# Linear attention's queries multiplied by two heads at once, the features' high part over their low part, against sums with high and low side by side

## The chip, the cores and the metric

One core of one Trainium2 chip runs the whole program. Its engines are TensorE (PE), VectorE (DVE), ScalarE (ACT), GpSimd (POOL) and SyncE (SP, which here issues the DMAs). The metric is the device time of one execution in microseconds. Three executions of the kernel before took 955.29, 956.08 (the median) and 1325.11 us.

## What is computed

Two kinds of layers alternate, each behind a layer norm and with a residual: A, B, A, B over x of 2048 rows and 512 columns. A is linear attention with 32 heads of 16 columns, B a hidden layer of 1792 with relu. All weights and the input are float32.

```
def A(x):                          # x: 2048 x 512
    q, k, v = x @ wqkv             # 32 heads of 16
    pq, pk = q @ w_phi, k @ w_phi  # per head
    phi_q = concat(softmax(pq), softmax(-pq))   # 32 features of a head
    phi_k = concat(softmax(pk), softmax(-pk))
    kv = phi_k.T @ v;  z = sum(phi_k)           # per head: 32 x 16, 32
    o = (phi_q @ kv) / (phi_q @ z + 1e-6)
    return o @ wo
def B(x):
    return relu(x @ w1) @ w2
x = x + A(norm(x)); x = x + B(norm(x)); x = x + A(norm(x)); x = x + B(norm(x))
```

## The kernel before

Rows are handled in 16 chunks of 128; two chunks make a tile of 256 rows for layer B. TensorE multiplies float16 operands. A float32 operand is split into a high float16 part and a low one (the rest after rounding), and a product is made of three matmuls, high x high, high x low, low x high (`PAIRS`).

A layer A needs two passes. In the first, `keys` and `values` project each chunk (`project`, line 656; results `pk`, `pv`), `feature_map` makes the features, and `gather` adds the outer products of features and values to the sums of all heads (`kv`). `query` projects the queries (`pq`) and stores them. `summary` then masks the sums (line 989), splits them into `rhs0` (high) and `rhs1` (low): for each group of four heads a matrix of 128 features and 68 columns, 64 for the four heads' values and 4 for their denominators. In the second pass `look` loads a chunk's queries, makes their features `p16` (high and low, 1024 columns each), and a transposing DMA turns these into `pT`: 8 blocks of high parts and 8 of low ones, a block being four heads' 128 features by 128 rows. `numerators` (line 1079) multiplies, in two halves of four groups; each group takes three matmuls of 68 columns that add up in PSUM (`pn`). DVE adds the guard to the denominators, inverts them and multiplies (lines 1087, 1090, 1091) into `o`. `turn` splits `o` (ACT line 570, POOL line 573) into `n_o`, and a DMA (line 584) transposes it to `oT`; the first two chunks of a layer are transposed on PE instead (`fast`). `back_project` multiplies by `wo` (`pw`), then come the norm and layer B: `ph` are hidden sums, `py` outputs. Most tiles of layer B use seven products instead of eight (line 1495); ACT copies partial hidden sums out of PSUM there (`sn`, line 1508) before PE adds the next product. The second pass of a layer runs inside layer B's steps: `sides` puts the numerators and the back projection of a later chunk between the hidden matmuls of an earlier tile. In the first layer, the second layer's keys and values are also made there.

The opening: `wk` is first multiplied by the per-head matrix (`fold`). The raw weight `st_k` arrives in three pieces (two row blocks, one, one). PE transposes its sixteen 128x128 blocks (line 1805) into four banks by column group, ACT and DVE copy them (`wT_k`, lines 1811 and 1812), PE multiplies (`pf_k`, line 1847), ACT and DVE round and split the result (`wk_h`, `wk_l`). The scale of that split comes from the sum of squares of the raw weight (ACT line 391, `sb_k` on PE), through DVE, a power of -0.5 on POOL (line 410) and DVE (`root`). Chunks 0 to 3 of the first layer have their normalised rows transposed on PE (`tr_a`, line 599), all others by DMA (`xT<-n_a`).

Work is first listed as tasks with what they read and write; then each engine's order is taken from the table `ORDER`: a string for each engine, whose digits say which of the tasks that are left comes next. Each engine, and SP with its DMAs, runs its tasks strictly in that order, waiting where an operand is not there.

## Time and profile before

| | |
|---|---|
| median of three executions | 956.08 us (955.29 to 1325.11) |
| the profiled execution | 955.23 us, its span 953.5 us |
| mean granted clock of TensorE | 1.00 |
| DVE, ACT, POOL busy | 72%, 62%, 65% of the span |
| DMA | 183.39 MB, mean 192 GB/s; the main queue's packets take 73.2% of 16 engines' span |

In rows of the profile, a group's entry reads: line, engine, operation, output <- inputs, shapes, count | busy us, mean ns of one | idle time of the engine before them and who ended it. Rows of the chain and of the timeline begin with the start and the length in us. A matmul's own length includes the time in which it drains while the next one runs, so the distance between starts is what it costs PE. PEld is PE's weight load.

### The profile page before, as it was taken

To read this page: it belongs to the slowest core of one execution; us is meant where nothing else is said; L and a number is where in the kernel's file an instruction comes from. 1 tells how busy PE (TensorE), PEld (TensorE's weight loads), DVE (VectorE), ACT (ScalarE), POOL (GpSimd) and SP (SyncE) were. 2 spreads that over 40 slices of the span, in tenths; PEclk is the share of its full clock that TensorE was granted. 3 is DMA by queue.
4 is the path that set the end of the run, shared out by engine and by line. 5 is a ranking of instruction groups with operands and counts; after the bars stand their busy time and mean duration, and the time that the engine had idled before them with its cause. 6 is when DMAs were issued, how large, how long until landed. Compare 5 with 4: busy or idle time off the path is not lost.

```text
span 953.5 us, 23741 instructions
## 1 busy us (share of the span) xinstructions
PE 944.3 (99%) x9364; PEld 657.6 (69%) x9364; DVE 685.9 (72%) x1419; ACT 593.4 (62%) x1193; POOL 622.0 (65%) x666
## 2 busy tenths in 40 slices
PE   8999999999999999999999999999999999999998
PEld 5544545665675666667677875566666989888997
DVE  7999888677768768776476678986887665555445
ACT  8999888754564646455266555566566566565553
POOL 2697966768975847665177747256557888786554
PEclk9999999999999999999999999999999999999999
DMA  9488647569878598967849663688999977765442
GB/s 340 127 263 190 176 122 187 124 143 211 235 169 241 152 225 222 228 167 206 198 146 273 232 221 91 194 217 209 251 215 254 242 170 170 195 169 154 142 140 79
DMA packets 251840, 183.39 MB, mean 192 GB/s; under 512 B 180688, under 2 KB 188112, under 8 KB 251728
## 3 DMA queue, kind: packets, MB, share of 16 engines
q1 hardware_dynamic: 251728, 181.87, 73.2%
q8 instruction: 73, 1.20, 0.5%
q14 instruction: 39, 0.32, 0.1%
HBM read 108.30 MB, written 30.15 MB: 145 GB/s over the span
## 4 chain that ended last, share of the span: by engine, by line
PE 96%; ACT 1%; DMA 1%; DVE 0%; issue 0%; POOL 0%; POOLq 0%; SPq 0%; DVEq 0%
PE ph L1495 24%; PE py L1614 15%; PE py L1684 13%; PE pw L656 9%; PE pv L656 9%; PE pq L656 9%; PE pk L656 9%; PE ph L1575 4%; PE pn L1079 2%; PE kv L864 1%; DMA oT<-n_o 0%; DMA st_k<-in_A_wqkv_dram 0%; PE pv L843 0%; PE pf_q L1847 0%; PE tr_a L599 0%
## 5 line engine op out<-in xcount | busy, mean ns | idle before, releaser
L1508 ACT ACTIVATE sn<-ph 128x128 f32<-128x128 f32 x294 | 80.6, 275 | 152.6 <-PE ph L1495 149.5
L1614 PE MATMUL py<-w,h 128*128 128x512 f16 x690 | 174.2, 379 | 0.0
L1495 PEld LDWEIGHTS <-s 128*128 128x128 f16 x2352 | 151.4, 98 | 26.0 <-issue 1.3
L656 PEld LDWEIGHTS <-xT 128*128 128x128 f16 x900 | 87.0, 98 | 98.9 <-issue 1.0
L1495 PEld LDWEIGHTS <-w 128*128 128x128 f16 x1764 | 111.0, 98 | 13.2 <-DVE h L1225 0.6
L1495 PE MATMUL ph<-yT,s 128*128 128x128 f16 x1176 | 97.6, 219 | 0.9 <-DVE ph L1514 0.9
L1495 PE MATMUL ph<-yT,w 128*128 128x128 f16 x1176 | 97.6, 219 | 0.0
L1514 DVE TENSOR_TENSOR ph<-ph,sn 128x128 f32<-128x128 f32 x98 | 29.3, 299 | 94.5 <-PE ph L1495 48.2
L1614 PEld LDWEIGHTS <-h 128*128 128x128 f16 x690 | 61.4, 98 | 48.3
L771 POOL TENSOR_TENSOR p_q<-e_q,p_q 128x1024 f16<-128x1024 f32 x32 | 70.7, 2210 | 28.5 <-ACT p_q L767 28.5
L771 POOL TENSOR_TENSOR p_k<-e_k,p_k 128x1024 f16<-128x1024 f32 x30 | 66.7, 2222 | 24.2 <-ACT p_k L767 23.9
L656 PE MATMUL pk<-wk_h,xT 128*128 128x512 f16 x256 | 81.5, 379 | 0.0
L656 PE MATMUL pw<-wo_h,oT 128*128 128x512 f16 x256 | 81.2, 379 | 0.2 <-DMA oT<-n_o 0.2
L656 PE MATMUL pv<-wv_h,xT 128*128 128x512 f16 x256 | 81.2, 379 | 0.0
L760 POOL TENSOR_TENSOR e_k<-e_k,fm_k 128x1024 f32<-128x1024 f32 x30 | 59.3, 1977 | 32.3 <-ACT fm_k L752 32.1
L1519 DVE TENSOR_TENSOR ph<-ph,sn 128x256 f32<-128x256 f32 x98 | 41.9, 427 | 32.6 <-PE ph L1495 32.1
L1684 PEld LDWEIGHTS <-h 128*128 128x128 f16 x648 | 59.1, 98 | 7.5 <-issue 0.5
L656 PEld LDWEIGHTS <-oT 128*128 128x128 f16 x384 | 36.6, 98 | 39.9 <-DMA oT<-n_o 0.7
L1291 POOL TENSOR_TENSOR w<-r 128x256 f32<-128x256 f32 x41 | 32.5, 793 | 43.9 <-ACT r L1287 43.8
L656 PE MATMUL pq<-wq_h,xq 128*128 128x512 f16 x168 | 56.8, 379 | 0.2 <-ACT qs L933 0.2
L1684 PE MATMUL py<-w,h 128*128 128x256 f16 x324 | 53.0, 273 | 0.3 <-POOL w L1291 0.3
L1225 DVE SCALAR_TENSOR_TENSOR h<-ph,h 128x512 f16<-128x512 f32 x58 | 39.3, 681 | 18.8 <-ACT h L1222 18.8
(285 smaller groups left out, 2438.0 us busy)
## 6 DMA issues: line engine op xcount, KB each, us to landing
s<-s_dram SPq DMA_DIRECT2D x98, 512.0 KB, 4.5
q_dram<-qs SPq DMA_DIRECT2D x28, 256.0 KB, 3.2
ql<-q_dram SPq DMA_DIRECT2D x28, 256.0 KB, 3.8
u<-t_dram SPq DMA_DIRECT2D x13, 512.0 KB, 5.5
xt_dram<-xT SPq DMA_DIRECT2D x21, 256.0 KB, 4.4
xq<-xt_dram SPq DMA_DIRECT2D x21, 256.0 KB, 3.3
xe<-in_A_x_dram SPq DMA_DIRECT2D x16, 256.0 KB, 4.3
x<-in_A_x_dram SPq DMA_DIRECT2D x16, 256.0 KB, 5.0
```

The lines of the kernel that those rows point to most:

```text
L656: nc.tensor.matmul(pm.ap, xT.ap[:, a, k, :], W.ap[b][:, k, :], start=(k == 0 and i == 0), stop=(k == KC - 1 and i == 2))
L760: (nc.vector if fast else nc.gpsimd).tensor_tensor(e3, e3, sm.unsqueeze(2).to_broadcast([P, 2 * n, DH]), op=ALU.mult)
L771: (nc.vector if fast else nc.gpsimd).tensor_sub(part16(1, cols), part16(1, cols, ef), part16(0, cols))
L1225: add(DVE, 0.607, lambda: nc.vector.scalar_tensor_tensor(h[1].ap, at(), 0.0, h[0].ap, op0=ALU.max, op1=ALU.subtract), reads=[ph, h[0]], wr ...
L1291: nc.gpsimd.tensor_sub(rf.ap[:, :2, :], r.ap.rearrange("p (a b) -> p a b", a=4)[:, ::3, :], block(1).unsqueeze(1).to_broadcast([P, 2, P]))
L1495: nc.tensor.matmul(at(r), weight_of(i, b, kk, s, summed), rows_of(y, i, a, kk), start=(first and kk == 0 and n == 0), stop=(kk == 1 and n ...
L1508: nc.scalar.activation(saved(i), at(2), AF.Copy)
L1514: add(DVE, 0.27, lambda: nc.vector.tensor_tensor(at(3), at(1), saved(2), op=ALU.add), reads=[(ph, 1), (sn, 2)], writes=[(ph, 3)], boost=10 ...
L1519: add(DVE, 0.40, lambda: nc.vector.tensor_tensor(wide(ph), wide(ph), wide(sn), op=ALU.add), reads=[(sn, 0), (sn, 1)], writes=[(ph, 0), (ph ...
L1575: nc.tensor.matmul(at()[:, j, cs.start * P:cs.stop * P], W1.at(b, k, slice(f * P, (f + 1) * P)), yT.ap[:, cs, a, k, :], stop=(k == KC - 1 ...
L1614: nc.tensor.matmul(py.ap, h[a].ap.rearrange("p j t -> p (j t)")[:, cols], W2.at(b, fs[j], slice(0, D)), start=(begins and j == k == 0), st ...
L1684: nc.tensor.matmul(py.ap[:, 256 * r:256 * r + 256], left[a], right[b], start=(s == 0 and r == 0 and k == 0), stop=(last and k == 2 and not ...
```

## The change

Numerators. The features of the queries are laid out so that one transposed block holds two heads: 64 rows of high parts over 64 rows of low parts, 16 blocks for a chunk. `rhs` has, for each pair of heads, the sums twice over on the partitions (once for the high, once for the low features) and 68 columns: 34 of the sums' high part (32 values and 2 denominators) beside 34 of their low part. One matmul of a block gives (high + low) x high in the left 34 columns and (high + low) x low in the right 34; DVE adds the two sides by a reduction. So 16 matmuls of 68 columns take the place of 24, in three banks (6, 5 and 5 pairs) instead of two. The division is no longer taken from PSUM: after the join, ACT scales the denominators, POOL adds the guard, DVE inverts, POOL multiplies; in the second layer from chunk 10 on DVE does both POOL steps. The first two chunks of a layer (`numerators_at_once`) add the two sides on PE instead, with two matmuls of 34 columns for each pair into one place, 32 for a chunk, and divide from PSUM as before. `spread` reads the heads from tiles with 34 columns to a pair. The masks and the matrix that doubles the sums over the halves of the partitions are built for pairs in the opening (two more ACT copies and a DVE reduction, while the first weight is still on its way).

Opening. The transposes of `st_k` are made in four units of four, one bank each; each unit is copied by one instruction of 512 columns (DVE, ACT, DVE, DVE). The power of -0.5 is replaced by integer arithmetic on DVE (`root`). Chunks 2 and 3 are transposed by DMA (`fast=c < 2`).

Order. All five strings of `ORDER` are new. The core of the diff:

```diff
@@ ORDER, PE @@
-        "0000222222110104100001100070088006600413318011593473108302a0302901a02211013517002060013GG00E1D4420133140"
...
+        "0000222200000100007b090077000440300115307015810209302901a302110135006001612031F0514BB2A24031033003304706"
...
@@ root @@
         def bound():
+            total = pb.ap[:, :1]
             if sq.n > 1:
+                total = m.ap
                 nc.vector.tensor_reduce(m.ap, pb.ap[:, :sq.n], axis=AX.X, op=ALU.add)
-            nc.vector.tensor_scalar(m.ap, m.ap if sq.n > 1 else pb.ap[:, :1], 2.0 ** -80, None, op0=ALU.max)
+            if name == "phi":
+                nc.vector.tensor_scalar(m.ap, total, 2.0 ** -80, None, op0=ALU.max)
+                total = m.ap
+            nc.vector.tensor_scalar(m.ap.bitcast(I32), total.bitcast(I32), -0.5, float(0x5F3759DF),
+                                    op0=ALU.mult, op1=ALU.add)
+            nc.vector.tensor_scalar(pw.ap.bitcast(I32), m.ap.bitcast(I32), 0x7F800000, None, op0=ALU.bitwise_and)
 
         add(PE, 0.23, sums, reads=[sq], makes=[pb])
-        add(DVE, 0.3 if sq.n > 1 else 0.12, bound, reads=[pb], writes=[m])
-        add(POOL, 0.515, lambda: nc.gpsimd.tensor_tensor(m.ap, m.ap, nhalf, op=ALU.pow), writes=[m])
-        add(DVE, 0.12, lambda: nc.vector.tensor_scalar(pw.ap.bitcast(I32), m.ap.bitcast(I32), 0x7F800000, None,
-                                                       op0=ALU.bitwise_and), reads=[m], writes=[pw])
+        add(DVE, 0.12 * (2 + (name == "phi")) + 0.15 * (sq.n > 1), bound, reads=[pb], writes=[m, pw])
...
@@ spread @@
-        src = lambda: x.ap[:, first:first + n]
+        pairs = hasattr(x, "of_heads")
+        src = (lambda: x.ap[:, :, :32]) if pairs else lambda: x.ap[:, first:first + n]
+        side_of = lambda i: n16.at()[:, i * n:(i + 1) * n].rearrange("p (g d) -> p g d", d=32) if pairs else \
+            n16.at()[:, i * n:(i + 1) * n]
 
         def hi():
             n16.ap = n16.make()
-            nc.scalar.activation(n16.at()[:, :n], src(), AF.Copy)
+            nc.scalar.activation(side_of(0), src(), AF.Copy)
 
         add(ACT, 0.085 + n / 1140, hi, reads=[x], makes=[n16])
-        add(POOL, 0.14 + n / 523, lambda: nc.gpsimd.tensor_sub(n16.at()[:, n:], src(), n16.at()[:, :n]),
+        add(POOL, 0.14 + n / 523, lambda: nc.gpsimd.tensor_sub(side_of(1), src(), side_of(0)),
             reads=[x], writes=[(n16, "l")])
...
@@ f32_tile, feature_map @@
+        if side == "b":
+            return plan.buf("xnb", lambda: fr.tile([P, H // 2, RW // 2], F32, name=name, **plan.slot("xnb"))
+                            .rearrange("p g d -> p (g d)")[:, :D])
...
-                return (p16.ap[:, j, cols] if x is None else x).rearrange(
-                    "p (h s f) -> p h s f" if x is None else "p (s h f) -> p h s f", s=2, f=DH)
+                if x is not None:
+                    return x.rearrange("p (s g c) -> p g s c", s=2, c=2 * DH)
+                return p16.ap.rearrange("p j c -> p (j c)").rearrange("p (g j s c) -> p j g s c", j=2, s=2, c=2 * DH)[:, j]
...
@@ summary @@
-        rhs[l] = r = [plan.buf(f"rhs{j}", partial(const.tile, [P, NG, RW], F16, name=f"rhs{j}_{l}", tag=f"rhs{j}"))
-                      for j in range(2)]
+        rhs[l] = r = plan.buf("rhs", partial(const.tile, [P, H // 2, RW], F16, name=f"rhs_{l}", tag="rhs"))
...
             def hi(tv=tv, g=g, i=i):
                 if i == 0:
-                    for b in r:
-                        b.ap = b.make()
-                nc.scalar.activation(r[0].ap[:, g, :], tv(), AF.Copy)
+                    r.ap = r.make()
+                nc.scalar.activation(r.ap[:, g, :RW // 2], tv(), AF.Copy)
 
...
@@ numerators @@
+    PARTS = (range(0, 6), range(6, 11), range(11, 16))
+
     def numerators(l, c, i, tag):
+
+        n = f"{l}_{c}"
+        if c < CPT:
+            return numerators_at_once(l, c, i, tag)
+        if i == 0:
+            heads[l, c] = plan.buf("xnb", lambda: fr.tile([P, H // 2, RW // 2], F32, name=f"o_{n}", **plan.slot("xnb")))
+            heads[l, c].of_heads = lambda: heads_of(0, 32)
+        of, pT, r, eps = heads[l, c], looking[l, c], rhs[l], guards[l, c]
+        heads_of = lambda a, b: of.ap[:, :, a:b].rearrange("p g (h f) -> p g h f", h=2)
+        for part in ((0,), (1, 2))[i]:
+            pn = bank(tag if part < 2 else "n", f"pn_{n}_{part}")
+            pairs, at = PARTS[part], lambda pn=pn, part=part: pn.ap[:, :len(PARTS[part]) * RW]
+
+            def go(pn=pn, pairs=pairs, at=at):
+                pn.ap = pn.make()
+                blocks = pT.ap.rearrange("p j g t -> p (j g) t")
+                for k, g in enumerate(pairs):
+                    nc.tensor.matmul(at()[:, k * RW:(k + 1) * RW], blocks[:, g, :], r.ap[:, g, :], start=True, stop=True)
+
+            def joined(part=part, pairs=pairs, at=at):
+                if part == 0:
+                    of.ap = of.make()
+                nc.vector.tensor_reduce(of.ap[:, pairs.start:pairs.stop, :],
+                                        at().rearrange("p (g j d) -> p g d j", j=2, d=RW // 2), axis=AX.X, op=ALU.add)
+
+            add(PE, 0.032 * len(pairs), go, reads=[pT, r], makes=[pn])
+            add(DVE, 0.1 + len(pairs) * RW / 930, joined, reads=[pn], makes=[(of, part)] if part == 0 else [],
+                writes=[] if part == 0 else [(of, part)])
+        if i == 0:
+            return
+        den = lambda: of.ap[:, :, 32:34]
+        quick = l == 1 and c >= 10
+        e, engine = (DVE, nc.vector) if quick else (POOL, nc.gpsimd)
+
+        def level():
+            nc.scalar.activation(den(), den(), AF.Copy, scale=1.0 / PHI)
+
+        def guarded():
+            engine.tensor_tensor(den(), den(), eps.ap.rearrange("p (g h) -> p g h", h=2), op=ALU.add)
+
+        def divide():
+            o = heads_of(0, 32)
+            engine.tensor_tensor(o, o, den().unsqueeze(3).to_broadcast([P, H // 2, 2, DH]), op=ALU.mult)
+
+        add(ACT, 0.18, level, reads=[], writes=[of])
+        add(e, 0.12 if quick else 0.31, guarded, reads=[eps], writes=[of], lock=quick)
+        add(DVE, 0.36, lambda: nc.vector.reciprocal(den(), den()), writes=[of])
+        add(e, 0.66 if quick else 1.08, divide, writes=[of], lock=quick)
+
+    def numerators_at_once(l, c, i, tag):
 
...
+            blocks = pT.ap.rearrange("p j g t -> p (j g) t")
+            for k, g in enumerate(pairs):
+                for j in range(2):
+                    nc.tensor.matmul(at()[:, k, :], blocks[:, g, :], r.ap[:, g, j * RW // 2:(j + 1) * RW // 2],
+                                     start=(j == 0), stop=(j == 1))
 
...
@@ the opening @@
-    st_k = load_piece(wqkv_v[1], "st_k", cuts=(2, 1, 1), late=300)
+    st_k = load_piece(wqkv_v[1], "st_k", cuts=(2, 1, 1), late=60)
...
+        def unit(i, ks, gs, n):
+
+            pt = pts[n] = bank(t_banks[n], f"wt_{name}{n}")
+            width = cuts[i] * P
+            cs = slice(ks.start * P, ks.stop * P)
+
+            def go():
+                pt.ap = pt.make()
+                for j, g in enumerate(gs):
+                    for m, k in enumerate(range(KC)[ks]):
+                        nc.tensor.transpose(pt.ap[:, j * width + m * P:j * width + (m + 1) * P],
+                                            f32_piece(src)[:, k, g * P:(g + 1) * P], ident)
+
+            def copy():
+                if n == 0:
+                    wT.ap = wT.make()
+                (nc.scalar.copy if copies[n] == ACT else nc.vector.tensor_copy)(
+                    f32_piece(wT)[:, gs.start:gs.stop, cs], pt.ap.rearrange("p (g c) -> p g c", c=width))
+
+            add(PE, 0.48, go, reads=[(src, i)], makes=[pt], after=active[-1:])
+            add(copies[n], 0.47 if copies[n] == ACT else 0.61, copy, reads=[pt], makes=[(wT, i)] if n == 0 else [],
+                writes=[] if n == 0 else [(wT, i)])
+
         for i, ks in enumerate(parts_of(cuts)):
             if len(cuts) > 1:
-                for g in range(4):
-                    turned(i, g, ks, active[-1:])
-                for g in range(4):
-                    copied(i, g, ks)
+                for gs in ((range(2), range(2, 4)) if cuts[i] == 2 else (range(4),)):
+                    unit(i, ks, gs, len(pts))
...
-    fold(st_k, Wk, "k", ("h", "h", "kv0", "kv1"), ("n", "y0", "kv0", "y1"), (ACT, DVE, ACT, DVE), "y1",
+    fold(st_k, Wk, "k", ("h", "h", "kv0", "kv1"), ("n", "y0", "kv0", "y1"), (DVE, ACT, DVE, DVE), "y1",
...
-            front_norm(0, c, early.pop(c), fast=c < 4, after=paced[:1] if c > 1 else [])
+            front_norm(0, c, early.pop(c), fast=c < 2, after=paced[:1] if c > 1 else [])
```

What the new order does at three places. ACT in the opening, from the copies of the transposed key weight to the first `wk_h`. Before:

```order
L391 ACTIVATE wk_l,sq_k<-st_k 128x1024
L1811 COPY wT_k<-wt_k_221 128x128
L391 ACTIVATE wk_l,sq_k<-st_k 128x512 x2
L1811 COPY wT_k<-wt_k_211 128x128
L604 ACTIVATE xT_0_265<-tr_a_0_234 128x512
L1811 COPY wT_k<-wt_k_221 128x128
L391 ACTIVATE wv_l,sq_v<-st_v 128x1024 x2
L438 ACTIVATE wk_h<-pf_k_249,s_k 128x512
L438 ACTIVATE wk_h<-pf_k_270,s_k 128x512
```

and now:

```order
L397 ACTIVATE wk_l,sq_k<-st_k 128x1024
L397 ACTIVATE wk_l,sq_k<-st_k 128x512
L397 ACTIVATE squares,sq_phi<-phi 128x64
L650 ACTIVATE xn_a_0_230<-xe_179,stat_a_0_201 128x512
L397 ACTIVATE wk_l,sq_k<-st_k 128x512
L1906 COPY wT_k<-wt_k_215 128x2x256
L618 ACTIVATE xT_0_254<-tr_a_0_240 128x512
L397 ACTIVATE wv_l,sq_v<-st_v 128x1024
L449 ACTIVATE wk_h<-pf_k_261,s_k 128x512
L397 ACTIVATE wv_l,sq_v<-st_v 128x1024
L449 ACTIVATE wk_h<-pf_k_272,s_k 128x512
```

The two halves of the value weight's squares (`sq_v`) stood ahead of all four `wk_h`; now the second half stands behind the first `wk_h`. On PE the sums for the value weight (`sb_v`) stand ahead of the first keys in both, and eight of the query weight's sixteen transposes have moved in among the first keys' matmuls.

SP, the DMAs behind the opening. Before:

```order
L497 DMA w_2_147<-in_B_w_dram 128x1792
L548 DMA xe_376<-in_A_x_dram 128x512
L497 DMA w_last<-in_B_w_dram 128x1792
L497 DMA w_4_154<-in_B_w_dram 128x2x512
L939 DMA q_dram<-qs_0_576 128x512
L584 DMA_TRANSPOSE xT_4_585<-n_a_4_561 128x8x128
```

and now:

```order
L508 DMA w_1_147<-in_B_w_dram 128x1792
L508 DMA w_2_148<-in_B_w_dram 128x1792
L508 DMA w_last<-in_B_w_dram 128x1792
L598 DMA_TRANSPOSE xT_2_458<-n_a_2_433 128x8x128
L559 DMA xe_469<-in_A_x_dram 128x512
L508 DMA w_3_149<-in_B_w_dram 128x1792
L598 DMA_TRANSPOSE xT_3_509<-n_a_3_482 128x8x128
```

The first transposing DMA was chunk 4's; chunks 2 and 3 now have one each ahead of it.

POOL around the heads `o` of chunk 8 in the first layer (`ts`, `xn_b` and `seconds` are sums for layer B, `stat` is a norm's power). Before:

```order
L771 TENSOR_TENSOR p_q_9_3747<-e_q_9_3503,p_q_9_3747 128x1024
L1151 TENSOR_TENSOR ts_3_3628<-xn_b_7_3619,ts_3_3628 128x256
L1151 TENSOR_TENSOR xn_b_6_3559<-xn_b_6_3559,ts_3_3628 128x256
L636 TENSOR_TENSOR stat_a_2_3829<-stat_a_2_3829,nhalf 128x1
L573 TENSOR_TENSOR n_o_8_3826<-o_8_3750,n_o_8_3826 128x512
```

and now:

```order
L789 TENSOR_TENSOR p_q_9_3681<-e_q_9_3490,p_q_9_3681 128x16x64
L1119 TENSOR_TENSOR o_8_3696<-o_8_3696,eps_q_8_3468 128x16x2
L1216 TENSOR_TENSOR ts_3_3600<-xn_b_7_3581,ts_3_3600 128x256
L1123 TENSOR_TENSOR o_8_3696<-o_8_3696 128x16x32
L653 TENSOR_TENSOR stat_a_2_3763<-stat_a_2_3763,nhalf 128x1
L1453 TENSOR_TENSOR seconds_3499<-seconds_3499 128x256
L587 TENSOR_TENSOR n_o_8_3792<-o_8_3696,n_o_8_3792 128x512
```

One instruction of POOL made the low part of the heads; now the guard and the product stand ahead of it, with other work between them. On PE, between this chunk's last numerator matmul and its back projection stood 90 matmuls of 128 columns, 24 of 512 and 24 of 68; now 78 of 128, 24 of 512 and 16 of 68.

163 lines of the change are left out of this document (81 added, 82 removed).

## The prediction

> **What bounds the kernel now.** I read the busy times first, then the chain of work that ended last, then the waits of TensorE, and then single stretches.
>
> ```profile
> span 953.5 us, 23741 instructions
> ...
> PE 944.3 (99%) x9364; PEld 657.6 (69%) x9364; DVE 685.9 (72%) x1419; ACT 593.4 (62%) x1193; POOL 622.0 (65%) x666
> ...
> PE 96%; ACT 1%; DMA 1%; DVE 0%; issue 0%; POOL 0%; POOLq 0%; SPq 0%; DVEq 0%
> ```
>
> TensorE (PE) is busy 99% of the span, and the chain that ended last is 96% PE. Its waits are eleven, one to two each; these are the first two and the last:
>
> ```profile
> PE warm L1864 <- DVE ones L329: 1.1, 1, 1.1
> PE ph L1495 <- DVE ph L1514: 0.9, 2, 0.5
> ...
> PE tr_a L599 <- ACT xn_a L633: 0.2, 1, 0.2
> ```
>
> Only matmul time removed from PE, or one of these few waits removed, can shorten the run. Busy PE time is inflated, since matmuls overlap; the price of one is the distance between starts, which long runs of one kind in the chain show:
>
> ```profile
> 26.75 2.59 PE pv L656 x12
> 180.61 2.62 PE ph L1575 x24
> 270.80 1.34 PE ph L1495 x24
> 148.22 1.50 PE pn L1079 x48
> L1079 PE MATMUL pn<-rhs,pT 128*128 128x68 f16 x768 | 33.1, 194 | 0.0
> ```
>
> That is 216 ns for 512 columns, 109 ns for 256, 56 ns for 128 and 31.2 ns for 68. The whole program's numerators are 768 matmuls of 68 columns: 768 x 31.2 = 24.0 us.
>
> **The change: numerators.** For 28 of the 32 chunk visits, 24 matmuls of 68 columns become 16 of 68 columns: 28 x 16 x 31.2 = 14.0 us. For the other four (chunks 0 and 1 of each layer) there are 32 matmuls of 34 columns. No row has 34 columns. Upper bound: 31.2 ns, the 68-column row. Lower bound: the rows above lie on a straight line, (216 - 109) / 256 = 0.42 ns for a column and 2.5 ns fixed, and 34 columns on it give 17 ns. I take 26 ns, nearer to the 68-column row, since each matmul still has its own weight load: 128 x 26 = 3.3 us, bounds 2.2 and 4.0. Saved: 24.0 - 14.0 - 3.3 = **6.7 us**, bounds 7.8 and 6.0.
>
> The Trainium skill ("TensorE: Matmul & The Clock Gate", "Wait — 56ns, not 53.3ns?") has starts never closer than about 25 ns however few the columns; by that the 128 would take 3.2 us by my estimate, and the sum would be 6.8 us. The 68-column row, above that floor, can't test it.
>
> **What DVE, ACT and POOL take over.** Before, a chunk's two halves each leave PSUM through three DVE instructions, 164 + 253 + 424 = 841 ns. After, DVE joins the two sides in three reductions, ACT scales the denominators, POOL adds the guard, DVE inverts, POOL multiplies (DVE does both POOL steps in the second layer from chunk 10 on, 6 chunks).
>
> ```profile
> L1087 DVE SCALAR_TENSOR_TENSOR dn<-pn,eps_q 128x16 f32<-128x16 f32 x64 | 10.5, 164 | 8.1 <-PE pn L1079 7.9
> L1090 DVE RECIPROCAL dn<-dn 128x16 f32<-128x16 f32 x64 | 16.2, 253 | 2.2
> L1091 DVE TENSOR_TENSOR o<-pn,dn 128x256 f32<-128x256 f32 x64 | 27.1, 424 | 2.3
> L967 DVE TENSOR_REDUCE kvs<-kv 128x231 f32<-128x462 f32 x2 | 1.3, 636 | 0.6 <-PE kv L864 0.6
> L748 ACT ACTIVATE eps_q<-fm_q 128x32 f32<-128x32 f32 x32 | 7.1, 222 | 1.5 <-DVE fm_q L731 1.3 <-DVE dn L1087 0.2
> L740 POOL TENSOR_TENSOR fm_q<-fm_q 128x32 f32<-128x32 f32 x32 | 9.4, 293 | 38.2 <-ACT fm_q L736 38.1
> L732 DVE RECIPROCAL fm_q<-fm_q 128x32 f32<-128x32 f32 x32 | 11.3, 353 | 1.1
> L757 POOL TENSOR_TENSOR e_q<-e_q,fm_q 128x512 f32<-128x512 f32 x32 | 33.9, 1060 | 1.6
> L570 ACT ACTIVATE n_o<-o 128x512 f16<-128x512 f32 x28 | 17.4, 622 | 4.4 <-DVE o L1091 3.9 <-DMA oT<-n_o 0.6
> L573 POOL TENSOR_TENSOR n_o<-o,n_o 128x512 f16<-128x512 f32 x28 | 32.4, 1158 | 15.2 <-ACT n_o L570 15.2
> oT<-n_o SPq DMA_TRANSPOSE x28, 3.5
> ...
> 4.53 0.15 DVE L629 TENSOR_SCALAR stat_a<-stat_a 128x1 f32<-128x1 f32 x1
> 5.35 0.21 DVE L638 TENSOR_SCALAR stat_a<-stat_a 128x1 f32<-128x1 f32 x1 [0.67 <-POOL stat_a L636]
> ...
> 4.77 0.55 POOL L636 TENSOR_TENSOR stat_a<-stat_a,nhalf 128x1 f32<-128x1 f32 x1 [1.31 <-DVE stat_a L629]
> ```
>
> The reduction over 462 elements takes 636 ns, so 340 elements cost about 0.5 us and 408 about 0.56. After the last numerator matmul the chain is then 0.5 + 0.22 + 0.29 + 0.35 + 1.06 = 2.4 us where it was 0.84; with three more hand-overs between engines at 0.1 us each it is 1.9 us longer. (A hand-over: DVE below ends at 4.68, POOL takes 4.77 to 5.32, DVE goes on at 5.35.) What follows is unchanged: 0.62 + 1.16 + 3.5 = 5.3 us, so 8.0 us in all, 8.4 with the later hand-overs, until the transposed heads have landed. The cost on PE is nothing as long as PE has that much other work between a chunk's last numerator and its back projection. At the place that the order shows for chunk 8 of the first layer, these are 78 matmuls of 128 columns, 24 of 512 and 16 of 68: 78 x 0.056 + 24 x 0.216 + 16 x 0.031 = 10.0 us. It was 11.0 us (90, 24 and 24). The cover exceeds the chain by 1.6 us there, and this is one of the tightest places; if it were gone, each such chunk would cost PE what the chain lacks. On POOL, 22 chunks x (0.29 + 1.06) add 30 us to 622, so it stays far from being the bound; DVE's change, 28 x (1.56 + 0.35 - 1.68) = 6 us and the six chunks' own guard and product, is as harmless. One new wait has something behind it: ACT's scaling waits for DVE's third join, and behind it in ACT's order stand copies of the hidden layer's sums, which PE's next accumulation there waits for. Waits of PE after the opening, 2.7 us in six of the eleven rows of its list, may so shrink or grow with the new order: cost taken 0, bounds -3 (all of them gone) and +6 (two times as many more).
>
> **The opening.** Until the first keys, ACT sets the pace:
>
> ```profile
> 10.56 2.08 ACT wv_l L391 x4
> 12.64 1.49 ACT wk_h L438 x3
> ...
> 15.71 0.33 PE tr_a L599
> L1811 ACT COPY wT_k<-wt_k 128x128 f32<-128x128 f32 x4 | 1.1, 273 | 0.0
> L1811 ACT COPY wT_k<-wt_k 128x256 f32<-128x256 f32 x2 | 0.8, 376 | 0.0
> L1811 ACT COPY wT_q<-wt_q 128x512 f32<-128x512 f32 x4 | 2.4, 655 | 0.0
> ```
>
> The key weight's scale waited for the squares and then for a round trip over POOL, after which ACT was in the middle of the value weight's 2.08 us of squares. The change makes ACT's six copies (4 x 0.27 + 2 x 0.38 = 1.9 us, about 1.2 as they overlap) one of 0.65, puts half of the value weight's squares behind the first part of the key weight, and takes POOL's power out of the root (its place is a DVE instruction of about 0.15 us). In PE's list of waits four rows fall between its first transpose and chunk 1's, 1.8 us (0.5, 0.5, 0.6 and the 0.2 quoted last), and starts of single transposes were late besides. ACT gains 0.6 us, and eight transposes of the query weight move up into what is left of the waits. I take **0.9 us** gained, bounds 0 (the sums for the value weight, which stand ahead of the first keys, end as late as before) and 2.2 (no wait left).
>
> **Chunks 2 and 3 by DMA.** Their normalised rows are no longer transposed on PE:
>
> ```profile
> 6.85 0.66 PE L599 MATMUL tr_a<-ident,xn_a 128*128 128x128 f32 x4
> 25.09 0.80 ACT L633 ACTIVATE xn_a<-xe,stat_a 128x512 f32<-128x512 f32 x1
> 31.63 0.38 PE L656 MATMUL pk<-wk_h,xT 128*128 128x512 f16 x1
> L570 ACT ACTIVATE n_a<-xn_a 128x512 f16<-128x512 f32 x26 | 16.3, 625 | 4.1 <-DMA xT<-n_a 3.8
> L573 POOL TENSOR_TENSOR n_a<-xn_a,n_a 128x512 f16<-128x512 f32 x26 | 30.3, 1167 | 27.1 <-ACT n_a L570 27.1
> xT<-n_a SPq DMA_TRANSPOSE x26, 3.3
> DMA to landing us min/median/max: 2.0/3.5/6.5
> ```
>
> Four take about 4 x 0.11 us, so PE saves **0.9 us**. But chunk 2's keys, at 31.63 before, could now start at 31.63 - 0.9 - 0.44 = 30.3. Its rows were normalised by 25.9, and about 0.9 earlier now; then come a weight's split on ACT (0.5, a third of the 1.49 above), the rounding (0.63), POOL's rest (1.17) and the transposing DMA (3.3): 25.0 + 5.6 = 30.6, 30.9 with hand-overs, 31.4 with one more such step on ACT ahead of it. I take a wait of PE of **1.0 us**, bounds 0 and 4 (a landing in 6.5 us). Behind that wait stand all later matmuls, so nothing hides it.
>
> **The sum** is made against the profiled execution, 955.23 us (span 953.5 and 1.7 around it), 0.85 below the median of 956.08 and 0.06 below the fastest run, 955.29. 955.2 - 6.7 - 0.9 - 0.9 + 1.0 + 0 = **947.7 us**, 0.8% less: inside the 2% that is about what a measurement of this kernel can tell from no change.
>
> **The rivals.**
>
> 1. *The heads come late* (slower). Place: the stretches where PE has 10.0 to 11.7 us of matmuls between a chunk's last numerator and its back projection; counted like chunk 8's, there are nine (10.1, 10.4, 10.8, 10.9, 11.0, 11.2, 11.4, 11.6, 11.7). For it: the chain now crosses POOL twice more, in order, and chunk 8's guard, product and rest have two half-size sums, a power and others between them; the power alone takes 0.55 of the 1.6 us, and the sums come near the rest at a little over half of the 512-element product's 1.06 each. Against it: PE waited for heads only 0.2 us before. At a chain of 12.0 us the nine lose 1.9 + 1.6 + 1.2 + 1.1 + 1.0 + 0.8 + 0.6 + 0.4 + 0.3 = 8.9 us: 956.6 us. It is slower than before from about 11.9 us on; for 2% slower, 974 us, the chain must reach some 13.5 us and others of the 28 chunks must wait too.
>
> 2. *The opening gives nothing and chunks 2 and 3 wait longer*: 947.7 + 0.9 + 2 = 950.6 us. For it: ACT and DVE are about 90% busy until 137 us, so a late row is not made up.
>
> ```profile
> 22.20:137.00 114.80, 114.80 (x760) 59.13 (x760) 103.02 (x192) 104.77 (x161) 90.67 (x65) 1.00 0.66 178
> ```
>
> 3. *The order also removes old waits*: opening 2.2, later waits -3: 955.2 - 6.7 - 0.9 - 2.2 + 0 - 3 = 942.4 us.
>
> 4. *Weight loads set the pace of narrow matmuls*, so that dropping 192 pairs saves more: at the 98 ns that one load is shown for, 192 x 0.098 = 18.8 us: 955.2 - 18.8 - 0.9 - 0.9 + 1.0 = 935.6 us. The 68-column row, 31.2 ns with a load for each matmul, speaks against it. The Trainium skill ("TensorE: Matmul & The Clock Gate", "Back-to-back issue gap") states about 81 ns for a pair at 128 columns, by which, my estimate, the 192 would save 15.6 us; the trace has 56 ns.
>
> ```profile
> L1495 PEld LDWEIGHTS <-w 128*128 128x128 f16 x1764 | 111.0, 98 | 13.2 <-DVE h L1225 0.6
> ```
>
> **How the numbers follow.** Forecast 62%; rival 1 16%; rival 2 12%; rival 3 8%; rival 4 2%. The forecast's own bounds, not all at one end at once, are 944.5 to 951.5. With rivals 2 and 3 and the nearer part of rival 1 the range is **943.5 to 954.5**. Faster by over 2% (below 936.1): rival 4, 0.02. Slower by over 2% (above 974.3): a fifth of rival 1, 0.03. Within: 0.95.
>
> **What would show it.** Right: 576 numerator matmuls, 448 of them at 31 ns and 128 near 26; PE's busy time down by about 7 us; one wait of about 1 us of PE on chunk 2's transposed rows, and its keys at about 31.3 us; PE still at 99%. Wrong: PE waiting several us in total for transposed heads, with POOL's product between (rival 1); 68-column matmuls at another distance than 31 ns; or waits of PE that the order put at places where no step of the change lies.

## The result, and the profile after

The changed kernel took 950.98 us in the median of six executions, against 956.75 us for the kernel before on the same chip; the ratio is 0.9937, with a 95% interval of 0.992 to 0.9954. One execution of each, 2674.05 and 1325.11 us, lies far outside and is left out of the ratio. The profiled execution of the change took 949.48 us, its span 947.8 us. The prediction was 947.7 us, with a range of 943.5 to 954.5. In two later groups of runs the change took 950.29 and 950.1 us (ratios 0.9921 and 0.9923, below). By the medians of each group the change saves 5.8, 7.5 and 7.8 us, and between the two profiles 5.7; the forecast had 7.5, counted from 955.2 us, where the kernel before has medians of 956.3 to 958.0 in the later groups.

The page of the change, the lines that answer to those of before; the last is the chain that ended last:

```profile
span 947.8 us, 23368 instructions
...
PE 937.4 (99%) x9164; PEld 650.3 (69%) x9164; DVE 701.1 (74%) x1372; ACT 596.2 (63%) x1218; POOL 648.8 (68%) x702
...
PE 90%; DMA 3%; DVE 2%; POOL 2%; ACT 1%; issue 1%; SPq 0%; POOLq 0%; DVEq 0%; ACTq 0%
```

PE's busy time fell by 6.9 us (944.3 to 937.4) and the span by 5.7. PE is still 99% busy, but the chain is now 90% PE where it was 96%: it runs over DMAs, DVE and POOL in more places. (That is where the chain passes, not time that PE stood still.) The list of PE's waits in the change (total in us, times, longest) has 6.7 us in twelve rows, where the kernel before had 5.6 in eleven; these are four of them:

```profile
PE ph L1560 <- DMA s<-s_dram: 1.1, 3, 0.5
PE wt_k L1900 <- DMA st_k<-in_A_wqkv_dram: 1.1, 2, 0.8
...
PE py L1749 <- POOL w L1356: 0.7, 2, 0.3
...
PE pw L673 <- DMA oT<-n_o: 0.2, 1, 0.2
```

The two waits of before on ACT's squares of the key and value weight (0.5 and 0.6 us) are gone. New is the first row: three times PE reaches a group of the hidden layer before the sums of its weights have been fetched (`s`, SP's issues at L1518). The last row is the one wait on transposed heads in this profile, as short as before; the change's third profile has 0.8 us there.

The numerators in the timeline of PE (start, duration, instruction); the row behind each group shows where the next work starts:

```profile
146.06 1.36 PE L1145 MATMUL pn<-rhs,pT 128*128 128x34 f16 x48
147.27 0.38 PE L673 MATMUL pq<-wq_h,xq 128*128 128x512 f16 x1
...
193.26 0.48 PE L1098 MATMUL pn<-rhs,pT 128*128 128x68 f16 x10
193.58 0.81 PE L1679 MATMUL py<-w,h 128*128 128x512 f16 x3
```

48 matmuls of 34 columns take 147.27 - 146.06 = 1.21 us, 25.2 ns each; ten of 68 columns take 0.32 us, 32 ns each.

Two points of time divide what was won. Chunk 2's keys started at 31.63 us before and start at 30.24 now, 1.4 earlier; the last matmul started at 949.88 before and starts at 943.97 now, 5.9 earlier. So the opening brought 1.4 us and everything behind it 4.5.

### The profile page after: what moved, and what is told of

The parts are those of the page before. It is cut to its first block, busy times and chain, and to the rows that moved or that the text cites. A ratio compares the mean times of both kernels' runs of the same rounds, so it can differ in the third digit from the quotient of the medians.

```text
span 947.8 us, 23368 instructions
## 1 busy us (share of the span) xinstructions
PE 937.4 (99%) x9164; PEld 650.3 (69%) x9164; DVE 701.1 (74%) x1372; ACT 596.2 (63%) x1218; POOL 648.8 (68%) x702
## 4 chain that ended last, share of the span: by engine, by line
PE 90%; DMA 3%; DVE 2%; POOL 2%; ACT 1%; issue 1%; SPq 0%; POOLq 0%; DVEq 0%; ACTq 0%
PE ph L1560 22%; PE py L1679 14%; PE py L1749 11%; PE pv L673 8%; PE pk L673 8%; PE pq L673 8%; PE pw L673 8%; PE ph L1640 4%; DMA s<-s_dram 2%; PE pn L1098 1%; PE kv L882 1%; DMA xq<-xt_dram 0%; DMA yT<-n_b 0%; DMA oT<-n_o 0%; DMA st_k<-in_A_wqkv_dram 0%
## 5 line engine op out<-in xcount | busy, mean ns | idle before, releaser
L1560 PEld LDWEIGHTS <-w 128*128 128x128 f16 x1764 | 110.6, 98 | 12.4 <-DVE h L1290 1.0
L1103 DVE TENSOR_REDUCE o<-pn 128x170 f32<-128x340 f32 (+1 forms) x84 | 42.9, 528 | 12.9 <-PE pn L1098 12.6
```

The costliest lines, as they stand in the source:

```text
L1103: nc.vector.tensor_reduce(of.ap[:, pairs.start:pairs.stop, :], at().rearrange("p (g j d) -> p g d j", j=2, d=RW // 2), axis=AX.X, op=ALU.add)
L1560: nc.tensor.matmul(at(r), weight_of(i, b, kk, s, summed), rows_of(y, i, a, kk), start=(first and kk == 0 and n == 0), stop=(kk == 1 and n ...
```

## The experiments

"From chunk 2's keys to the end" below is the time in a run's trace from the first matmul of chunk 2's keys to the start of the last matmul: 918.25 us before, 913.74 in the change. It leaves the opening out, which differs from one execution to the next (last section). Each group of runs has its own runs of the kernel before on its chip.

| run | median us | ratio to before, 95% | chunk 2's keys to the end |
|---|---|---|---|
| the change again | 950.29 | 0.9907 to 0.9934 | 913.48 |
| eight more matmuls in a visit | 957.32 | 0.9981 to 1.0003 | 921.87 |
| second product in the heads' chain | 958.09 | 0.9995 to 1.0015 | 921.58 |
| second product off the chain | 954.32 | 0.9945 to 0.9975 | 918.57 |
| numerators in the old order, division on DVE | 989.95 | 1.0315 to 1.036 | 955.01 |
| the same, division spread as in the change | 988.5 | 1.0319 to 1.0347 | 950.01 |
| squares moved back | 950.98 | 0.991 to 0.9946 | 913.92 |
| nine moves against late waits | 949.11 | 0.9894 to 0.9922 | 912.75 |
| seven of them and one other | 947.78 | 0.9882 to 0.9922 | 911.62 |
| these eight, one of them further ahead, and two more | 949.44 | 0.991 to 0.9938 | 911.84 |
| the change a third time | 950.1 | 0.9909 to 0.9938 | 915.22 |
| the seven and one again, same chip | 950.06 | 0.9904 to 0.9937 | 912.25 |

### Is the gain PE's matmul time?

> The changed kernel once more, beside the next three, so that they are compared on one chip. Both theories: 951.0 us (949.5 to 952.5), ratio to the kernel before 0.994.

> The changed kernel, but in each of the 28 chunk visits with joined sides eight of the sixteen numerator matmuls are issued twice, into the same place, so that PE has the old count of 24 again and the result is unchanged. Theory A (the change gains by PE's matmul time alone, one for one, and its new order costs a few us of waits elsewhere): 28 x 8 x 31.2 ns = 7.0 us more, 958.0 us (957 to 959), so slower than the kernel before by about 1 us. Rival B (the waits that grew after 160 us belong to chains of other engines that now set the pace, so that longer PE work is partly swallowed by them): 3 us of the 7.0 are swallowed, 955 us.

```diff
-                for k, g in enumerate(pairs):
+                for k, g in [*enumerate(pairs), *enumerate(pairs[:(3, 3, 2)[part]])]:
```

957.32 us against 950.29: 7.0 us more, as 28 x 8 x 31.2 ns has it. Nothing of it was swallowed (rival B falls), and with the old count of matmuls the gain is gone (0.9981 to 1.0003). So the run pays added matmul time of PE in full. (The profile, of the slowest of the twelve executions, has 8.1 to 8.4 us more from chunk 2's keys to the end than the change's first two.) It also tells what the rest of the change, the opening and the waits of the new order together, is worth beside the numerators: between 1.8 us won and 0.3 lost.

### The heads' chain, and POOL's queue

> The changed kernel, with POOL's product of the heads followed by a second product of the same size, by one, in the 22 chunk visits where POOL makes it; the result is unchanged. It makes each of these chains 1.06 us longer. In the trace of the changed kernel the transposed heads of these chunks land 0.16 to 7.4 us ahead of the back projection that reads them; nine of them less than 1.06 us ahead. Theory A (heads have little to spare but are on the path nowhere by more than 0.4 us): what the nine lack, 0.89 + 0.54 + 0.90 + 0.38 + 0.26 + 0.11 + 0.10 and less, 3.2 us more, 954.2 us (953 to 955.5). Rival B (the heads have cover, and rows ahead of them in the queues decide): below 952. Rival C (POOL's order is so full that each product delays what stands behind it): 957 or more.

```diff
             engine.tensor_tensor(o, o, den().unsqueeze(3).to_broadcast([P, H // 2, 2, DH]), op=ALU.mult)
+            if not quick:
+                one = ones[:, :H].rearrange("p (g h) -> p g h", h=2)
+                engine.tensor_tensor(o, o, one.unsqueeze(3).to_broadcast([P, H // 2, 2, DH]), op=ALU.mult)
```

> The changed kernel with a second product of the heads by one on POOL as in the run that lengthened their chain, in the same 22 chunk visits, but put behind the rest of the heads, where nobody waits for it; the result is unchanged. POOL has the same 23 us more. That run took 7.8 us more than the changed kernel. Theory A (what cost there was the chain: transposed heads late, 3.3 us of waits, and ACT's in-order queue held up by the rounding that waits for the product, with copies behind it that PE needs): at most 2 us more than the changed kernel, 952.3 us or less. Rival B (POOL's order is full, whatever stands in it delays the rest): 4 us more or over, 954.3 us or more.

```diff
+        def rest():
+            nc.gpsimd.tensor_sub(side_of(1), src(), side_of(0))
+            if pairs and name not in [f"o1_{c}" for c in range(10, 16)]:
+                o = src().rearrange("p g (h f) -> p g h f", h=2)
...
+                nc.gpsimd.tensor_tensor(o, o, one.unsqueeze(3).to_broadcast([P, H // 2, 2, DH]), op=ALU.mult)
```

In the chain the second product cost 7.8 us (958.09 - 950.29), off the chain 4.0 (954.32 - 950.29). By their numbers the theories on POOL's order hold, C in the first run (957 or more) and B in the second (954.3 or more), but the second only by 0.02 us, with executions between 952.19 and 956.69, and against the change's median of another group; by the two ratios to the kernel before (0.996 and 0.9921) it is 3.7 us. But the chain has its part too. The starts of PE's matmuls in the first of these runs show waits on transposed heads of 0.89, 1.05, 0.15, 0.17 and 1.00 us, 3.3 in all: that is what the slack of the change's heads had said, 3.2. The other 4.5 us are waits elsewhere. Here is one, in that run's timeline:

```profile
281.43 0.28 ACT L1576 ACTIVATE sn<-ph 128x128 f32<-128x128 f32 x1 [0.71 <-PE ph L1563]
281.82 1.06 POOL L1126 TENSOR_TENSOR o<-o,ones 128x512 f32<-128x512 f32 x1
...
282.91 0.63 ACT L584 ACTIVATE n_o<-o 128x512 f16<-128x512 f32 x1 [1.08 <-POOL o L1126]
...
285.15 0.26 ACT L1576 ACTIVATE sn<-ph 128x128 f32<-128x128 f32 x1
...
285.46 0.33 PE L1563 MATMUL ph<-yT,s 128*128 128x128 f16 x3 [0.38 <-ACT sn L1576]
```

ACT's rounding of the heads (L584) stands in ACT's queue and waits 1.08 us for POOL's extra product; behind it stand three more instructions and then the copy `sn` of the hidden layer's sums, and for that copy PE waits 0.38 us at 285.46. PE does not wait for the heads at all here; it waits for something that was queued behind them. ACT's list of waits in that run has the sum, 22.1 us in 16 places; the change has 5.1 us in 4 in its second profile and 4.3 in 3 in its first:

```profile
ACT n_o L584 <- POOL o L1126: 22.1, 16, 4.2
```

Off the chain the waits on heads shrink to 0.3 us, but fetches and rows that stand behind POOL's work are late instead:

```profile
PE ph L1566 <- DMA s<-s_dram: 1.8, 4, 0.8
PE pk L679 <- DMA xT<-n_a: 1.3, 1, 1.3
...
PE pw L679 <- DMA oT<-n_o: 0.3, 1, 0.3
```

The second row is the product's doing: the transpose of these rows is issued 3.56 us behind that of the heads, where it is 2.44 in the change, since POOL's product stands between. So 23 us more on an engine that is 68% busy cost about 4 us behind the heads, where no one waits for them, and about 4 more when they lengthened the chain.

### Could the numerators change without the new order?

> The kernel before with its own order on every engine, its own opening and its own transposes of chunks 2 and 3; only the numerators are changed, in the places where they stood: per half seven pairs of heads as matmuls of 68 columns that DVE joins, and the eighth pair as two of 34 columns that PE adds up; DVE does the whole division. PE then saves 28 x (10 x 31.2 - 4 x 25) = 5.9 us and loses 0.2 in the four other visits; DVE takes about 0.6 us more in each of 56 halves, 34 us in all. Theory A (matmul time alone): 5.7 us less than the kernel before, ratio 0.994. Rival B (heads and other rows then come late, and the new order is what keeps the gain): at most 2.5 us less, ratio 0.9975 or more.

```diff
+                if k < 7:
+                    nc.tensor.matmul(pn.ap[:, k * RW:(k + 1) * RW], blocks[:, g, :], r.ap[:, g, :], start=True, stop=True)
+                else:
+                    for j in range(2):
+                        nc.tensor.matmul(pn.ap[:, k * RW:k * RW + RW // 2], blocks[:, g, :],
+                                         r.ap[:, g, j * RW // 2:(j + 1) * RW // 2], start=(j == 0), stop=(j == 1))
...
+            nc.vector.tensor_reduce(of.ap[:, pairs.start:pairs.stop - 1, :],
+                                    pn.ap[:, :7 * RW].rearrange("p (g j d) -> p g d j", j=2, d=RW // 2), axis=AX.X, op=ALU.add)
+            nc.vector.tensor_copy(of.ap[:, pairs.stop - 1, :], pn.ap[:, 7 * RW:7 * RW + RW // 2])
```

(The diff is against the kernel before and leaves out the layouts, which are those of the change.) 989.95 us: 32 us slower than before. Theory A falls; rival B had the direction, but not the size. The groups of DVE in that run:

```profile
L1099 DVE TENSOR_REDUCE o<-pn 128x238 f32<-128x476 f32 x56 | 36.0, 642 | 2.8 <-PE pn L1092 2.8
L1108 DVE TENSOR_TENSOR o<-o 128x256 f32<-128x256 f32 x56 | 32.0, 571 | 1.9
L1103 DVE SCALAR_TENSOR_TENSOR o<-o,eps_q 128x16 f32<-128x16 f32 x56 | 24.0, 429 | 2.2
```

With 253 ns for the inversion and 182 for the eighth pair's copy a half takes 642 + 182 + 429 + 253 + 571 = 2077 ns on DVE in one piece, where it took 841: 1.24 us more in 56 places, twice what I had put down. The extra shows in PE's waits, on the hidden layer's sums that DVE adds up behind that piece and on the copies that ACT makes for them:

```profile
PE ph L1544 <- DVE ph L1563: 12.2, 14, 2.5
PE ph L1544 <- ACT sn L1557: 6.9, 8, 1.8
```

A part of the 32 us is in none of these waits: the granted clock of TensorE. In this run's profile it reads 0.50 for three stretches of 3.4 us, from 219.8, 291.4 and 728.4 us on, and in the next run's for two, from 217.7 and 238.2 us on; the change's three profiles have none from chunk 2's keys to the last matmul. In the 3.4 us ahead of each of the five PE had been busy for only 0.5 to 1.5 us. This is the start of the last one, in the next run's timeline:

```profile
238.21 0.61 PE L668 MATMUL pw<-wo_h,oT 128*128 128x512 f16 x1 [2.06 <-DMA oT<-n_o]
238.61 0.63 PE L668 MATMUL pw<-wo_l,oT 128*128 128x512 f16 x1
239.04 1.06 PE L668 MATMUL pw<-wo_h,oT 128*128 128x512 f16 x2
239.89 0.64 PE L668 MATMUL pw<-wo_l,oT 128*128 128x512 f16 x1
```

Matmuls of 512 columns start some 420 ns apart there, instead of 216. Summed over the matmuls that start at twice their distance, the clock costs 4.6 us in this run and 3.3 in the next. So a long wait of PE can cost a second time, behind its end.

The run above mixes the order with a longer DVE piece, so the next takes the division as the change spreads it.

> The kernel before with its own order, opening and transposes, and with the numerators exactly as in the change: three joined parts, the division over ACT, DVE and POOL. The parts stand where the two halves stood (the third behind the second); the scaling, the guard, the inversion and the product are put into the queues of ACT, POOL and DVE where the trace of the kernel before has them due, and what rounds the heads and sends them off moves behind the product; nothing on TensorE moves to make room. PE saves about 6.3 us of matmuls. By the trace of the kernel before the transposed heads landed 0.04 to 8.6 us ahead of the back projection; with a chain 1.9 us longer, 18 of the 28 chunks lack 0.01 to 1.86 us, 15.6 us in all. Theory A (in the old order the longer chain of the heads has no cover; the new order is what gives it): 957 - 6.3 + 15.6 = 966 us (960 to 972), slower than before. Rival B (matmul time decides, and the run before with the division on DVE was slow only for DVE's 2 us in one piece): 951 to 954 us, as fast as the change.

```diff
-                for gs in ((range(2), range(2, 4)) if cuts[i] == 2 else (range(4),)):
-                    unit(i, ks, gs, len(pts))
+                for g in range(4):
+                    turned(i, g, ks, active[-1:])
+                for g in range(4):
+                    copied(i, g, ks)
...
-            front_norm(0, c, early.pop(c), fast=c < 2, after=paced[:1] if c > 1 else [])
+            front_norm(0, c, early.pop(c), fast=c < 4, after=paced[:1] if c > 1 else [])
```

(The diff is against the change; besides, the order is that of before with six instructions inserted in each of 28 visits, and the square root goes over POOL again.) 988.5 us: the same 32 us, above the 960 to 972 of theory A, which has the direction and a part of the size:

```profile
PE pw L668 <- DMA oT<-n_o: 10.8, 7, 2.4
PE pw L668 <- DVE o L1098: 6.7, 4, 3.0
PE pq L668 <- DVE o L1098: 5.2, 5, 1.7
PE pn L1093 <- DVE o L1098: 2.7, 7, 0.8
```

10.8 us are transposed heads that come late, where 15.6 had been reckoned. The three rows below it, 14.6 us together, I had not thought of. The back projection `pw` and the query projections `pq` do not read the heads whose joining they wait for; they take their turn at the two PSUM banks "n" that the numerators' parts also use, and a part holds its bank until DVE has joined it. A third part in each visit is a third turn, and PE's next user of the bank waits for DVE's place in its queue.

### The opening

> The changed kernel, but on ACT the second half of the value weight's squares stands ahead of the key weight's four splits again, as in the kernel before. Its input lands at 10.2 us and DMA jitter, where the first split started at 10.6; the second half ran at 12.2 to 12.4 us in the changed kernel. Theory A (ACT's order set the pace of the opening): the splits wait until about 12.3 us less what the move itself saves, 0.3 to 1.7 us more, 950.6 to 952.0 us, and in the trace the first keys start 0.3 to 1.7 us later after the landing of the key weight's last piece than the 6.2 us of the changed kernel. Rival B (the value weight's sums set it in both kernels): first keys still at 6.2 us behind that landing, no difference.

```diff
+MOVES = {'ACT': [(52, 39)]}
...
+        for a, b in MOVES.get(engine, ()):
+            t = next(t for t in queue if t.at == a)
+            queue.remove(t)
+            queue.insert(next(i for i, u in enumerate(queue) if u.at == b), t)
```

(52 is the second half of the value weight's squares, 39 the first split of the key weight.) The medians, 950.98 and 950.29, do not tell the two apart. The trace does: ACT's first split of the key weight starts at 11.76 us instead of 10.64. (In the change the second half of the squares runs from 11.22 to 12.36; the 12.2 to 12.4 above is only its end.) The first keys start at 6.1 us behind the landing, as rival B had it, but stop after four matmuls, because the last split is late:

```profile
13.74 0.59 PE L679 MATMUL pk<-wk_h,xT 128*128 128x512 f16 x2
14.94 0.38 PE L679 MATMUL pk<-wk_l,xT 128*128 128x512 f16 x1 [0.60 <-DVE wk_l L465]
```

Chunk 2's keys then start 24.2 us behind the landing of the key weight's last piece, where the change has 23.2 in its first and third profile: 1.0 us, the size of theory A, though at another place. (The second has 23.8, with slow transposes ahead of the keys; see the last section.) By one profile of this run, ACT's order in the opening is worth about that.

### Are the late waits time that can be had?

> The changed kernel, with nine instructions or groups of them moved ahead on their own engines (three fetches on SP, two on DVE, two on ACT, one on POOL, one of PE's groups moved behind its neighbours), each so that one of eight late waits of PE after 270 us should vanish: 0.41 (sums fetched behind the second layer's piece), 0.34 (hidden rows behind a shift of exponents), 0.64 and 0.54 (sums fetched behind a transpose and a store), 0.32 (projection of queries), 0.37 (the rest of the heads behind a fold), 0.50 and 0.50 (folds), 3.6 us in all. Theory A (these are accidents of the new order, each on the path by itself): 2.5 to 3.6 us less, 947.4 to 948.5 us. Rival B (the same chains end late at the next place, PE only waits there): 0 to 1 us less, 950 to 951 us.

```diff
+MOVES = {'PE': [(3083, 3084)], 'DVE': [(1652, 1734), (4629, 4600)], 'ACT': [(4867, 4881), (4630, 4644)], 'POOL': [(3912, 3802)], 'SP': [(1246, 1237), (1718, 1668), (2086, 2033)]}
```

> The changed kernel with the moved instructions of the run before, except two moves that gave new waits there (the fetch of the sums ahead of a transpose of features, and the rest of the heads ahead of a fold on POOL); in place of the first, the fetch of a later chunk's logits, read 40 us later, is moved behind two fetches of the sums, out of a stretch where the DMA engines are 99% busy. Theory A (each late wait is on the path by itself): 2.2 to 3 us less than the changed kernel, ratio to the kernel before 0.9895 to 0.991. Rival B (the chains end late at the next place): no better than the run before, ratio 0.991 or more.

```diff
-MOVES = {'PE': [(3083, 3084)], 'DVE': [(1652, 1734), (4629, 4600)], 'ACT': [(4867, 4881), (4630, 4644)], 'POOL': [(3912, 3802)], 'SP': [(1246, 1237), (1718, 1668), (2086, 2033)]}
+MOVES = {'PE': [(3083, 3084)], 'DVE': [(1652, 1734), (4629, 4600)], 'ACT': [(4867, 4881), (4630, 4644)], 'SP': [(1246, 1237), (1939, 1744), (2086, 2033)]}
```

> The changed kernel with the moves of the run that moved fewer, and three more for waits of PE seen in that run's trace: 0.62 us for a transpose of features that stood behind the fetch of logits (the fetch goes further back, and PE takes the numerators one place later), 0.27 us for heads (the back projection goes behind two groups of the hidden layer). Theory A: 0.3 to 0.9 us less than that run, ratio to the kernel before 0.989 to 0.990. Rival B: no difference that can be measured, 0.990 to 0.991.

```diff
-MOVES = {'PE': [(3083, 3084)], 'DVE': [(1652, 1734), (4629, 4600)], 'ACT': [(4867, 4881), (4630, 4644)], 'SP': [(1246, 1237), (1939, 1744), (2086, 2033)]}
+MOVES = {'PE': [(3083, 3084), (1823, 1830), (3417, 3425)], 'DVE': [(1652, 1734), (4629, 4600)], 'ACT': [(4867, 4881), (4630, 4644)], 'SP': [(1246, 1237), (1939, 1731), (2086, 2033)]}
```

> The changed kernel again, on one chip with the next run. Both theories: ratio to the kernel before 0.992 to 0.994.

> The changed kernel with the seven moves that had given the lowest median (947.78 us), beside the changed kernel on the same chip. In the two profiles it took 1.9 to 2.1 us less from chunk 2's keys to the last matmul. Theory A (late waits that a move removes are time won): 1.5 to 2.5 us less than the changed kernel in the median, and again about 911.6 us from chunk 2's keys to the last matmul, where the changed kernel has 913.5 to 913.7. Rival B (the lowest median was an early landing of the key weight): no difference in the medians beyond 0.5 us.

(Each pair moves the first task ahead of the second on its engine, by the function in the diff above. The moved kernels differ in two more places: they fix the place of each buffer tagged `w2`, that of the fetched sums, when it is listed, and no longer make its fetch depend on the one listed ahead of it.) The moves did what they were made for: in the trace with nine of them the waits of 0.41, 0.34, 0.64, 0.54, 0.32, 0.37, 0.50 and 0.50 us are gone. But others came: 1.03 us on the transposed features that the fetch had been put ahead of, 1.01 us on the next sums, 0.51 us on a fold that the rest of the heads had been put ahead of, and 0.32 us at another group of the hidden layer. With these two moves undone and a fetch of logits put back, the waits on sums are down from 1.1 us to 0.2, and the one on features is gone, but the next chunk's features, whose transpose now stands behind that fetch of logits, are late (by starts 0.62 us):

```profile
PE pn L1105 <- DMA pT<-p_q: 0.5, 1, 0.5
...
PE ph L1567 <- DMA s<-s_dram: 0.2, 1, 0.2
```

In their four traces the moved kernels (the second and the last are one kernel) need 911.62 to 912.75 us from chunk 2's keys to the end, the change in its three profiles 913.48 to 915.22: 0.7 to 3.6 us less. The medians do not settle it. Seven and one gave 947.78 us and then, beside the change on one chip, 950.06 against 950.1. That last comparison was to decide between the two theories, and by its medians rival B holds. No version is shown to beat the change; whether 0 or 2 us are to be had in this way stays open.

## Why the prediction was right, and which of its steps were not

**Numerators, -6.7: right.** By the distances of all starts the 768 took 24.1 us; now the 448 take 14.4 (15.1 less two waits of 0.64 and 0.14 that end among them) and the 128 take 3.2. That is 6.5 us less. For 34 columns I had taken 26 ns between 17 and 31.2; they take 25.2. The straight line through the wider rows fails there by 8 ns. The Trainium skill ("TensorE: Matmul & The Clock Gate", "Wait — 56ns, not 53.3ns?") has starts never closer than about 25 ns; the trace agrees, with 25.2 for 34 columns. The run with eight more matmuls confirmed the price of the 68 columns from the other side, 7.0 us for 224. Rival 4, weight loads as the pace, is out.

**Transposes, -0.9: right**, 40 instead of 48 at 109 ns.

**The opening, -0.9: right in size.** Chunk 2's keys are 1.40 us earlier; four of the eight transposes are 0.44 of it, 0.95 is left. Counted from the landing of the key weight's last piece (7.1 us in both) it is the same. The run with the squares moved back puts 1.0 us on ACT's order alone.

**Chunk 2's rows, +1.0: wrong; there is no wait.** The timeline of the change, from the normalised rows to the keys:

```profile
23.31 0.81 ACT L650 ACTIVATE xn_a<-xe,stat_a 128x512 f32<-128x512 f32 x1
24.03 0.67 ACT L449 ACTIVATE wq_h<-pf_q,s_q 128x512 f16<-128x512 f32 x1
24.60 0.62 ACT L584 ACTIVATE n_a<-xn_a 128x512 f16<-128x512 f32 x1
...
25.29 1.16 POOL L587 TENSOR_TENSOR n_a<-xn_a,n_a 128x512 f16<-128x512 f32 x1 [5.06 <-ACT n_a L584]
...
26.48 1.34 SPq L598 DMA_TRANSPOSE xT<-n_a  x1
...
30.24 0.38 PE L673 MATMUL pk<-wk_h,xT 128*128 128x512 f16 x1
```

The transpose landed 3.2 us behind its issue, at 29.6, and PE came at 30.24. The step that failed is "normalised by 25.9, and about 0.9 earlier now": the rows were normalised by 24.1, 1.8 us earlier, since the new order moved them ahead on ACT by more than the opening gained. What I added behind it, 5.6 us, was right (5.5). The lower bound, 0, was the value.

**Later waits, 0 between -3 and +6: mis-sized; they cost 2.4 us.** From chunk 2's keys to the end 4.5 us were won; the numerators and the other four transposes are 6.5 + 0.4 = 6.9 of matmul time. The starts of PE's matmuls show the difference directly: distances that exceed the usual one of their shape by over 45 ns add up to 4.6 us in 11 places before and to 7.1 in 22 now, 2.5 us more. In the sum, -6.5 - 0.9 - 0.95 + 0 + 2.4 = -5.9, which is the distance of the two last matmuls, and 949.5 is the profiled time. So a wait of 1.0 that did not come stands against waits of 2.4 that did: that the sum lies within 1.6 us of the profile, and not 2.6, is luck.

**The heads.** The chain behind the last numerator matmul begins with the join of the third part, five pairs, and is 505 + 229 + 373 + 344 + 1051 = 2502 ns in the groups of the change; 2.4 us were predicted:

```profile
L1103 DVE TENSOR_REDUCE o<-pn 128x170 f32<-128x340 f32 x56 | 27.3, 505 | 8.6 <-PE pn L1098 8.5
...
L1123 POOL TENSOR_TENSOR o<-o 128x512 f32<-128x512 f32 x22 | 23.1, 1051 | 7.0 <-DVE o L1127 6.9
...
L1127 DVE RECIPROCAL o<-o 128x32 f32<-128x32 f32 x28 | 9.6, 344 | 0.9 <-POOL o L1119 0.3
L1119 POOL TENSOR_TENSOR o<-o,eps_q 128x32 f32<-128x32 f32 x22 | 8.2, 373 | 12.9 <-ACT o L1116 12.8
...
L1116 ACT ACTIVATE o<-o 128x32 f32<-128x32 f32 x28 | 6.4, 229 | 16.8 <-DVE o L1103 16.4
```

At chunk 8 of the first layer I had put the cover at 1.6 us more than the chain; its transposed heads land 1.3 us ahead of their use (issued at 279.91, landed 3.1 us later, read at 284.34). PE waits for heads 0.2 us in all in this profile and 0.8 in the third, so rival 1 did not come. But its price was wrong. I had counted the heads alone and set the point where the change turns slower at a chain of about 11.9 us, 3.5 more than forecast. The second product made it 1.06 us longer, and that run already stands at 0.9995 to 1.0015. What I left out is that ACT's queue stops at the rounding of the heads and keeps from PE what is queued behind it; I had named this for ACT's scaling of the denominators, but not for the rounding, and had put no price on either.

**"POOL stays far from being the bound": true, and no reason to call it harmless.** 23 us more on POOL, with no one waiting for them, cost about 4 us. That the 27 us which the change itself puts on POOL (622.0 to 648.8) have their part in the 2.4 us of waits is likely from this, but no run shows it: the moves against those waits settled nothing.

**What the prediction did not see** is what the new order is for. It entered the sum as "cost taken 0". The same numerators and the same division, set into the old order by hand, took 988.5 us where the change takes about 950. Of these 38 us the old opening has a small part, some 2 us by the terms above, and the clock about 3; most of the rest are back projections and query projections that waited for banks and heads. Another way of setting them into the old order was not tried, so 38 us is not the worth of the new order as such. But had the change come in this way, the forecast's sum would have missed by about that much.

## What to carry to other kernels

Where PE sets the pace, matmul time that is added is paid one for one, and what is removed is won as far as no new waits come: 6.9 us removed gave 4.5 here. Its price can be read from the starts of neighbouring shapes, but not far below them: 34 columns cost 25.2 ns, not the 17 of the line. What takes over the removed work must be priced by what stands behind it in its queue and by the banks that it holds, not by the busy share of its engine: the same numerators in the old order lost 32 us. Before such a change is called covered, take the slack of each chunk from the trace (landing against first use) and ask which instructions of other work stand behind the one that waits.
